# A spectral layer with two dense layers: inverse DFT constants split on chip, and a front in another order

## The chip, the cores and the metric

The kernel runs on one core of a Trainium2 chip. The metric is device time in microseconds (us). The kernel before takes 1214.83 us, the median of three runs (1214.05 to 1216.38). The engines are TensorE (PE; its weight loads are PEld), VectorE (DVE), ScalarE (ACT), GpSimd (POOL) and SyncE (SP), which here only issues transfers. DVE, ACT and POOL each take their instructions in the order in which they are written.

## The reference

The input `x` has 2 sequences of 3008 tokens with 256 features. A spectral layer comes first, then two dense layers on the 6016 tokens:

```
X  = rfft(x, axis=1)
Yr = Xr @ w_r - Xi @ w_i + b_r ;  Yi = Xr @ w_i + Xi @ w_r + b_i
Y  = soft threshold (0.01) of Yr and of Yi, each by itself
x  = irfft(Y, n=3008)
h  = x @ w_in ;   x = (h - tanh(h)) @ w_out
h  = x @ w_in2 ;  y = (h * clip(h + 3, 0, 6) / 6) @ w_out2
```

## The kernel before

A float32 operand is split into a high part `h` (rounded to the type that TensorE takes, float32r) and a low part `l`, and a product is three matmuls: h by h, h by l, l by h (`three_pass`, lines 119 to 122). The splitting is `split` (lines 115 to 117): ACT copies to the high part, DVE subtracts it from the source.

The transform of length 3008 is done in two steps, 47 by 64, and so has four matrices: `am` and `bm` forwards, `cm` and `dm` backwards. The spectral phase runs like this:

- `dft_a(i)`, i = 0 to 15 (8 for each sequence): 8 matmuls with `am` on one chunk of `x`, eviction from PSUM, and a store to DRAM (`s1`), issued by ACT. For sequence 0 the first four frequency groups are kept on the chip: they sit in partitions 96 to 127 of `xa`, and SP copies them into the ring buffer `bi_ring[0]` by 4 transfers (line 657).
- `dft_b(j)`, j = 0 to 23: two frequency groups, with the matrix `bm` (tile `bmt`, loaded in 6 groups of 256 KB), out of a ring of three buffers `bi_ring` that `load_bi` fills from `s1`. `dft_b(2)` is the first that needs `load_bi(1)` and the second group of `bm`.
- ACT and DVE split its result: `evict_b_hi` (ACT, `fh`), `evict_b_lo` (DVE, `fl`), `evict_b_neg` (ACT, a negated copy inside `fl`).
- `linear(j)`: 24 matmuls with the split weights `lwH`, `lwL`. Then `shrink` (bias and soft threshold: three operations of DVE, lines 349 to 351), `shrink_hi` (ACT, `sh`) and `shrink_lo` (DVE, `sl`).
- `dft_c(j)`: 12 matmuls with `cm` (two tiles, `cmH` and `cmL`, 6 groups of columns each), `evict_c` on ACT (`co`), and a store to `s2`. `dft_d` comes later.

The loop over t = 0 to 23 (line 679) issues `linear(t)`, `dft_c(t-2)`, `dft_b(t+2)` and, while there are chunks left, one `dft_a` for TensorE; and in this order for the other engines: `evict_c(t-2)`, `evict_b_hi(t+2)`, `shrink(t)`, `shrink_hi(t)`, `evict_b_lo(t+2)`, `evict_b_neg(t+2)`, three steps of weight decoding, `shrink_lo(t)`, the eviction and store of `dft_a`, loads, three more steps of decoding. The schedule is written by hand (`tc.manual_schedule`, line 615), so this is the order on each engine.

The weights of the dense layers come as 64-bit floats. `w_steps` (lines 164 to 210) rebuilds float32 out of the integer words and splits it, in small steps that are spread over the loop. A tile takes two operations on ACT (lines 174, 175), then on DVE lines 177, 187 and 199, for a tile of `w_in` also four small additions (lines 203 to 207), and its split one step of the next tile later (ACT line 184, DVE line 192). Tiles of `w_in` (896 columns in the split) and of `w_out` (512) alternate.

In the kernel before, `cm` comes from DRAM in both parts: line 626 loads a group's high and its low part, 256 KB each, on POOL's queue, behind a small copy (`gate`, line 624) that holds the load back until its turn.

The dense phase (`group`, lines 570 to 613) follows; the change does not touch it.

Of the kernel before, what the change touches and what calls it, by code (L numbers as in the profile page):

```python
# [20 lines left out]
K1 = 24  # L21
# [6 lines left out]
def dft_constants():  # L28
    def trig(idx, period):
        idx = np.asarray(idx, dtype=np.int64) % period  # L30
        a = 2.0 * np.pi * idx.astype(np.float64) / period
        c, s = np.cos(a), np.sin(a)
        s[(2 * idx) % period == 0] = 0.0
        c[(4 * idx) % period == 0] *= (2 * idx[(4 * idx) % period == 0]) % period == 0
        return c, s

    n1 = np.arange(N1)
    k1 = np.arange(K1)
    c, s = trig(n1[:, None] * k1[None, :], N1)
    am = np.zeros((N1, 2, K1, 2, 2))  # L40
    dm = np.zeros((K1, 2, 2, N1, 2))
    wt = np.where(k1 == 0, 1.0, 2.0) / SEQ
    for par in range(2):
        am[:, par, :, 0, par] = c
        am[:, par, 1:, 1, par] = -s[:, 1:]
        dm[:, 0, par, :, par] = (c * wt).T
        dm[1:, 1, par, :, par] = (-s * wt).T[1:]

    n2 = np.arange(N2)
    k2 = np.arange(N2)  # L50
    k = k1[:, None] + N1 * k2[None, :]
    sgn = np.where(k <= SEQ // 2, 1.0, -1.0)
    cb, sb = trig(n2[:, None, None] * k[None], SEQ)
    bm = np.zeros((2, N2, K1, 2, N2))
    bm[0, :, :, 0, :] = cb
    bm[1, :, :, 0, :] = sb
    bm[0, :, :, 1, :] = -sgn * sb
    bm[1, :, :, 1, :] = sgn * cb
    cm = np.zeros((2, N2, K1, 2, N2))
    ct = cb.transpose(2, 1, 0)  # L60
    st = sb.transpose(2, 1, 0)
    sg = sgn.T[:, :, None]
    cm[0, :, :, 0, :] = ct
    cm[1, :, :, 0, :] = -sg * st
    cm[0, :, :, 1, :] = st
    cm[1, :, :, 1, :] = sg * ct
    f = np.float32

    def round_r(v):
        u = v.astype(f).view(np.uint32)  # L70
        u = (u + np.uint32(0x7FF) + ((u >> np.uint32(12)) & np.uint32(1))) & np.uint32(0xFFFFF000)
        return u.view(f)

    am96 = np.zeros((96, 128))
    am96[0:94, 0:96] = am.reshape(94, 96)
    am96[0:94, 96:128] = am.reshape(94, K1, 4)[:, 0:8].transpose(0, 2, 1).reshape(94, 32)
    cm = cm.reshape(128, K1 * 128).astype(f)
    ch = round_r(cm)
    cl = round_r(cm - ch)
    return {  # L80
        "am": am96.astype(f),
        "bm": bm.reshape(128, K1 * 128).astype(f),
        "cm": np.stack([ch, cl], axis=1),
        "dm": dm.reshape(96, 94).astype(f),
    }

# [2 lines left out]
def spectral_moe_kernel(ctx: ExitStack, tc: tile.TileContext, x, w_r, w_i, b_r, b_i,  # L89
# [46 lines left out]
        W[nm, c] = pl.tile([128, 2, n], F32R, tag=f"w{kind}{c}", name=f"w{kind}{c}")  # L136
        return W[nm, c]

    A0 = 9
    NDEC = 13  # L140
    w_src = {"1i": w1i, "1o": w1o, "2i": w2i, "2o": w2o}
    w_order = [(nm, c) for c in range(8) for nm in ("1i", "1o")]
# [136 lines left out]
    def dft_a_out(i, banks_):  # L279
# [6 lines left out]
                act.activation(out=xt[:, 2 * g:2 * g + 2, :], in_=banks_[g], func=ACTF.Copy)  # L286
        act.dma_start(out=s1w[b][:, 4 * c:4 * c + 4, :], in_=xt[0:96])

    bi_t, xf_t, s_t = {}, {}, {}
    GB = 4  # L290

# [323 lines left out]
    with tc.manual_schedule():  # L615
# [6 lines left out]
        def load_cm(g, after):  # L622
            if g < 6:
                pool.tensor_copy(out=gate[0:1, 0:1], in_=after)
                for h, t in enumerate((cmH, cmL)):
                    pool.dma_start(out=t[:, 512 * g:512 * g + 512], in_=cm[:, h, 512 * g:512 * g + 512])

        sp.dma_start(out=amt, in_=am)
        for i in range(8):
            load_x(i)  # L630
        warm = ca.tile([128, 256], F32, name="warm")
        dve.memset(warm, 0.0)
        for _ in range(4):
            p = bank("h")
            pe.matmul(out=p[:, 0:256], lhsT=warm[:, 0:128], rhs=warm, start=True, stop=True)
        for r in range(3):
            pool.memset(x1[r][64:96], 0.0)
        dve.memset(three, 3.0)
# [3 lines left out]
            sp.dma_start(out=t, in_=w.rearrange("(h p) d -> p h d", p=128))  # L642
            lws.append(t)
        load_bm(0)
        load_x(8)
        w_load()
        for k, w in enumerate((b_r, b_i)):
            sp.dma_start(out=bias[64 * k:64 * k + 64, 0, :],
                         in_=w.rearrange("(o d) -> o d", o=1).broadcast_to([64, D]))
        for i in range(A0):  # L650
            dft_a(i)
            if i == 5:
                for k in range(2):
                    split(lwH[:, k], lwL[:, k], lws[k])
            if i == 7:
                for k in range(GB):
                    sp.dma_start(out=bi_ring[0][:, k, :], in_=xa[96 + k:128:8])
                bi_t[0] = bi_ring[0]
        load_x(9)
        load_bi(1)  # L660
        load_bm(1)
        load_x(10)
        w_load()
        sp.dma_start(out=dmt, in_=dm)
        for _ in range(5):
            w_step()
        wa_cm.__exit__(None, None, None)
        wpool["r"] = ctx.enter_context(tc.tile_pool(name="wr", bufs=1, side="right", reuse_waits="tile"))
        for j in range(2):
# [1 line left out]
            evict_b_hi(j)  # L671
            evict_b_lo(j)
            evict_b_neg(j)
            if j == 0:
                load_cm(0, xf_t[0][0].bitcast(F32)[0:1, 0, 64:65])
        load_bi(2)
        NP = K1
        a_next = A0
        for t in range(NP):
# [7 lines left out]
                evict_c(t - 2)  # L687
            if t + 2 < NP:
                evict_b_hi(t + 2)
            shrink(t)  # L690
            if t < NP - 1:
                shrink_hi(t)
# [6 lines left out]
            if t + 2 < NP:  # L699
                evict_b_neg(t + 2)  # L700
            for _ in range(3 if t < 10 else 2):
                if t > 1 and ptr["dec"] < NDEC:
                    w_step()
            shrink_lo(t)
            for nm in {20: ("b11", "b21"), 21: ("t1",), 22: ("t2", "b22")}.get(t, ()):
# [9 lines left out]
            if t % 2 == 0:  # L715
                load_bm(t // 2 + 2)
                load_cm(t // 2 + 1, s_t[t][0].bitcast(F32)[0:1, 0, 0:1])
            load_x(11 + t)
            if t == 0:
                w_load()  # L720
            if t % 2 == 1:
                load_bi((t + 1) // 2 + 2)
            for _ in range(3 if t < 10 else 1 + t % 2):
                if t > 1 and ptr["dec"] < NDEC:
                    w_step()
            if t == 14:
                load_din(0, din0)
# [122 lines left out]
```

## Time and profile before

| | |
|---|---|
| median of three runs | 1214.83 us |
| the profiled execution | 1212.14 us |
| its span (first to last instruction) | 1210.3 us |
| PE busy | 1185.4 us (98%) |
| DVE busy | 965.6 us (80%) |
| ACT busy | 875.2 us (72%) |
| POOL busy | 157.2 us (13%) |

The profile's page lists busy time over the whole span. The spectral phase is the first 170 us or so of it; the timeline lists single instructions, and a bracket at a row's end says how long the engine stood idle before it and what ended the wait. "PEclk" is the clock that TensorE was granted, as a share of its upper level of 2.4 GHz.

### The profile page before, as it was taken

To read this page: it belongs to the slowest core of one execution; us is meant where nothing else is said; L and a number is where in the kernel's file an instruction comes from. 1 tells how busy PE (TensorE), PEld (TensorE's weight loads), DVE (VectorE), ACT (ScalarE), POOL (GpSimd) and SP (SyncE) were. 2 spreads that over 40 slices of the span, in tenths; PEclk is the share of its full clock that TensorE was granted. 3 is DMA by queue.
4 is the path that set the end of the run, shared out by engine and by line. 5 is a ranking of instruction groups with operands and counts; after the bars stand their busy time and mean duration, and the time that the engine had idled before them with its cause. 6 is when DMAs were issued, how large, how long until landed. Compare 5 with 4: busy or idle time off the path is not lost.

```text
span 1210.3 us, 20904 instructions
## 1 busy us (share of the span) xinstructions
PE 1185.4 (98%) x7832; PEld 1164.5 (96%) x7832; DVE 965.6 (80%) x1820; ACT 875.2 (72%) x1827; POOL 157.2 (13%) x162
## 2 busy tenths in 40 slices
PE   7989999999999999999999999999999999999998
PEld 5888989999999999999999999999999999999998
DVE  2589988888988888888777787878787878787875
ACT  2576678777777777777777677777777777776765
POOL 0100000203020110202021402011020202020200
PEclk8899999999999999999999999999999999999999
DMA  9996621112232223120105530101010101010000
GB/s 292 284 308 187 205 87 44 41 70 74 92 105 74 75 75 100 57 82 25 51 1 196 178 111 1 52 1 52 1 52 1 53 1 52 1 29 24 14 14 26
DMA packets 47797, 96.52 MB, mean 80 GB/s; under 512 B 4352, under 2 KB 27488, under 8 KB 47696
## 3 DMA queue, kind: packets, MB, share of 16 engines
q1 hardware_dynamic: 41728, 74.09, 19.2%
q0 software_dynamic: 4032, 14.68, 3.8%
q10 hardware_dynamic: 1936, 6.42, 1.4%
q8 instruction: 61, 1.00, 0.3%
q14 instruction: 40, 0.33, 0.1%
HBM read 58.22 MB, written 36.44 MB: 78 GB/s over the span
## 4 chain that ended last, share of the span: by engine, by line
PE 73%; DVE 11%; ACT 11%; DMA 2%; issue 2%; SPq 0%; ACTq 0%; DVEq 0%
PE acc L122 13%; PE acc L120 13%; PE acc L121 13%; PE al L120 6%; PE al L121 6%; PE al L122 6%; PE be L122 3%; PE be L121 3%; PE be L120 3%; ACT gh L116 3%; DVE g L447 3%; PE ga L405 2%; DVE gl L117 2%; PE ga L121 1%; PE ga L122 1%
## 5 line engine op out<-in xcount | busy, mean ns | idle before, releaser
L117 DVE TENSOR_TENSOR gl<-g,gh 128x376 fp32r<-128x376 f32 x509 | 292.2, 574 | 149.6 <-ACT gh L116 123.2
L116 ACT ACTIVATE gh<-g 128x376 fp32r<-128x376 f32 x509 | 263.4, 517 | 176.7 <-DVE g L450 91.5
L122 PE MATMUL acc<-wo,gl 128*128 128x256 f32 (+1 forms) x768 | 215.9, 281 | 0.0
L121 PE MATMUL acc<-wo,gh 128*128 128x256 f32 (+1 forms) x768 | 215.8, 281 | 0.0
L120 PE MATMUL acc<-wo,gh 128*128 128x256 f32 (+1 forms) x768 | 215.6, 281 | 0.0
L120 PE MATMUL acc<-gh,wo 128*128 128x376 f32 x512 | 173.2, 338 | 0.0
L122 PE MATMUL acc<-gh,wo 128*128 128x376 f32 x512 | 171.0, 334 | 0.0
L121 PE MATMUL acc<-gl,wo 128*128 128x376 f32 x512 | 170.7, 333 | 0.0
L121 PEld LDWEIGHTS acc<-wo,gh 128*128 128x128 f32 (+1 forms) x768 | 143.0, 186 | 0.0
L122 PEld LDWEIGHTS acc<-wo,gl 128*128 128x128 f32 (+1 forms) x768 | 142.9, 186 | 0.0
L120 PEld LDWEIGHTS acc<-wo,gh 128*128 128x128 f32 (+1 forms) x768 | 142.8, 186 | 0.0
L414 POOL TENSOR_TENSOR bmt<-bmt 128x376 f32<-128x376 f32 x60 | 73.4, 1224 | 445.5 <-ACT bmt L407 331.2
L450 DVE SCALAR_TENSOR_TENSOR g<-e,c 128x376 f32<-128x376 f32 x192 | 118.5, 617 | 12.2 <-ACT e L449 7.5
L449 ACT ACTIVATE e<-c,three 128x376 f32<-128x376 f32 x192 | 116.7, 608 | 7.7 <-DVE c L596 7.5
L447 DVE TENSOR_TENSOR g<-c,e 128x376 f32<-128x376 f32 x189 | 114.5, 606 | 5.9 <-ACT e L446 3.4
L430 POOL TENSOR_TENSOR cmL<-bmt,cmH 128x376 fp32r<-128x376 f32 x60 | 64.9, 1082 | 324.8 <-ACT cmH L425 324.8
L446 ACT ACTIVATE e<-c 128x376 f32<-128x376 f32 x189 | 97.6, 516 | 10.0 <-DVE c L596 9.8
L120 PEld LDWEIGHTS acc<-gh,wo 128*128 128x128 f32 x512 | 96.3, 188 | 0.0
L121 PEld LDWEIGHTS acc<-gl,wo 128*128 128x128 f32 x512 | 96.2, 188 | 0.0
L122 PEld LDWEIGHTS acc<-gh,wo 128*128 128x128 f32 x512 | 96.1, 188 | 0.0
L586 ACT ACTIVATE s<-be 128x376 f32<-128x376 f32 x127 | 61.8, 487 | 40.5 <-PE be L122 39.9
L120 PE MATMUL al<-cmH,wi 128*128 128x376 f32 x256 | 87.3, 341 | 2.1 <-ACT s L582 0.3
(173 smaller groups left out, 2831.2 us busy)
## 6 DMA issues: line engine op xcount, KB each, us to landing
raw<-in_moe_w_in_dram SPq DMA_DIRECT2D x16, 512.0 KB, 3.9
raw<-in_moe_w_out_dram SPq DMA_DIRECT2D x16, 512.0 KB, 4.2
w2id<-wout SPq DMA_DIRECT2D x8, 896.0 KB, 4.7
wi<-w2id POOLq DMA_DIRECT2D x8, 896.0 KB, 4.9
y1d<-y SPq DMA_DIRECT2D x32, 188.0 KB, 2.0
bmt<-y1d SPq DMA_DIRECT2D x8, 752.0 KB, 4.5
s<-co SPq DMA_DIRECT2D x23, 256.0 KB, 4.6
bi_all<-s SPq DMA_DIRECT2D x11, 512.0 KB, 5.1
```

Source lines behind the costliest of these rows:

```text
L116: act.activation(out=hi, in_=src, func=ACTF.Copy)
L117: (lo_eng or dve).tensor_tensor(out=lo, in0=src, in1=hi.bitcast(F32), op=ALU.subtract)
L120: pe.matmul(out=out_ap, lhsT=lh, rhs=rh, start=start, stop=False, **kw)
L121: pe.matmul(out=out_ap, lhsT=lh, rhs=rl, start=False, stop=False, **kw)
L122: pe.matmul(out=out_ap, lhsT=ll, rhs=rh, start=False, stop=stop, **kw)
L414: eng.tensor_tensor(out=out, in0=a, in1=b, op=ALU.subtract)
L430: (eng or dve).tensor_tensor(out=l, in0=OPS[nm][0], in1=h.bitcast(F32), op=ALU.subtract)
L446: act.activation(out=e, in_=src, func=ACTF.Tanh)
L447: dve.tensor_tensor(out=g, in0=src, in1=e, op=ALU.subtract)
L449: act.activation(out=e, in_=src, func=ACTF.Relu, bias=three)
L450: dve.scalar_tensor_tensor(out=g, in0=e, scalar=6.0, in1=src, op0=ALU.min, op1=ALU.mult)
L586: act.activation(out=s5, in_=be, func=ACTF.Copy)
```

## The change

Three things change together.

1. `cm` is one float32 array in DRAM. `load_cm` loads a group of 256 KB into one of two buffers `cmf`, and a new function `split_cm(g)` splits it on ACT and DVE into `cmH` and `cmL`. It is called at t = 1, 3, 5, 7, 9 and 11, ahead of `shrink(t)`. The gate of the first group is now the first of the four copies into `bi_ring[0]`.
2. The front is in another order. `A0` is 8 instead of 9, so `dft_a(8)` moves into the loop, and the loop does one more `dft_a` (t = 0 to 7). The split of `lwH`, `lwL` moves from between the evictions of `dft_a` to behind them. On SP the four copies into `bi_ring[0]` come ahead of the two bias loads, `load_x(8)`, `load_bi(1)` and the first `w_load`. Eleven matmuls on a tile of zeros (`warm`) stand between `dft_a(7)` and `dft_b(0)`. `warm` has 240 columns instead of 256.
3. The five decoding steps ahead of the loop are gone; decoding starts at t = 1 instead of t = 2.

```diff
@@ -66,21 +66,13 @@
     cm[1, :, :, 1, :] = sg * ct
     f = np.float32
 
-    def round_r(v):
-        u = v.astype(f).view(np.uint32)
-        u = (u + np.uint32(0x7FF) + ((u >> np.uint32(12)) & np.uint32(1))) & np.uint32(0xFFFFF000)
-        return u.view(f)
-
     am96 = np.zeros((96, 128))
     am96[0:94, 0:96] = am.reshape(94, 96)
     am96[0:94, 96:128] = am.reshape(94, K1, 4)[:, 0:8].transpose(0, 2, 1).reshape(94, 32)
-    cm = cm.reshape(128, K1 * 128).astype(f)
-    ch = round_r(cm)
-    cl = round_r(cm - ch)
     return {
         "am": am96.astype(f),
         "bm": bm.reshape(128, K1 * 128).astype(f),
-        "cm": np.stack([ch, cl], axis=1),
+        "cm": cm.reshape(128, K1 * 128).astype(f),
         "dm": dm.reshape(96, 94).astype(f),
     }
 
@@ -136,7 +128,7 @@
         W[nm, c] = pl.tile([128, 2, n], F32R, tag=f"w{kind}{c}", name=f"w{kind}{c}")
         return W[nm, c]
 
-    A0 = 9
+    A0 = 8
     NDEC = 13
     w_src = {"1i": w1i, "1o": w1o, "2i": w2i, "2o": w2o}
     w_order = [(nm, c) for c in range(8) for nm in ("1i", "1o")]
@@ -286,6 +278,7 @@
                 act.activation(out=xt[:, 2 * g:2 * g + 2, :], in_=banks_[g], func=ACTF.Copy)
         act.dma_start(out=s1w[b][:, 4 * c:4 * c + 4, :], in_=xt[0:96])
 
+    cmf = {}
     bi_t, xf_t, s_t = {}, {}, {}
     GB = 4
 
@@ -622,17 +615,22 @@
         def load_cm(g, after):
             if g < 6:
                 pool.tensor_copy(out=gate[0:1, 0:1], in_=after)
-                for h, t in enumerate((cmH, cmL)):
-                    pool.dma_start(out=t[:, 512 * g:512 * g + 512], in_=cm[:, h, 512 * g:512 * g + 512])
+                cmf[g] = ca.tile([128, 512], F32, tag="cmf", bufs=2, name="cmf")
+                pool.dma_start(out=cmf[g], in_=cm[:, 512 * g:512 * g + 512])
+
+        def split_cm(g):
+            if g < 6:
+                sl = slice(512 * g, 512 * g + 512)
+                split(cmH[:, sl], cmL[:, sl], cmf[g])
 
         sp.dma_start(out=amt, in_=am)
         for i in range(8):
             load_x(i)
-        warm = ca.tile([128, 256], F32, name="warm")
+        warm = ca.tile([128, 240], F32, name="warm")
         dve.memset(warm, 0.0)
         for _ in range(4):
             p = bank("h")
-            pe.matmul(out=p[:, 0:256], lhsT=warm[:, 0:128], rhs=warm, start=True, stop=True)
+            pe.matmul(out=p[:, 0:240], lhsT=warm[:, 0:128], rhs=warm, start=True, stop=True)
         for r in range(3):
             pool.memset(x1[r][64:96], 0.0)
         dve.memset(three, 3.0)
@@ -642,28 +640,28 @@
             sp.dma_start(out=t, in_=w.rearrange("(h p) d -> p h d", p=128))
             lws.append(t)
         load_bm(0)
-        load_x(8)
-        w_load()
+        for i in range(A0):
+            dft_a(i)
+        for k in range(GB):
+            sp.dma_start(out=bi_ring[0][:, k, :], in_=xa[96 + k:128:8])
+        bi_t[0] = bi_ring[0]
         for k, w in enumerate((b_r, b_i)):
             sp.dma_start(out=bias[64 * k:64 * k + 64, 0, :],
                          in_=w.rearrange("(o d) -> o d", o=1).broadcast_to([64, D]))
-        for i in range(A0):
-            dft_a(i)
-            if i == 5:
-                for k in range(2):
-                    split(lwH[:, k], lwL[:, k], lws[k])
-            if i == 7:
-                for k in range(GB):
-                    sp.dma_start(out=bi_ring[0][:, k, :], in_=xa[96 + k:128:8])
-                bi_t[0] = bi_ring[0]
+        load_x(8)
+        load_bi(1)
+        w_load()
         load_x(9)
-        load_bi(1)
         load_bm(1)
+        sp.dma_start(out=dmt, in_=dm)
         load_x(10)
         w_load()
-        sp.dma_start(out=dmt, in_=dm)
-        for _ in range(5):
-            w_step()
+        load_cm(0, bi_ring[0][0:1, 0, 0:1])
+        for k in range(2):
+            split(lwH[:, k], lwL[:, k], lws[k])
+        for _ in range(11):
+            p = bank("h")
+            pe.matmul(out=p[:, 0:240], lhsT=warm[:, 0:128], rhs=warm, start=True, stop=True)
         wa_cm.__exit__(None, None, None)
         wpool["r"] = ctx.enter_context(tc.tile_pool(name="wr", bufs=1, side="right", reuse_waits="tile"))
         for j in range(2):
@@ -671,8 +669,6 @@
             evict_b_hi(j)
             evict_b_lo(j)
             evict_b_neg(j)
-            if j == 0:
-                load_cm(0, xf_t[0][0].bitcast(F32)[0:1, 0, 64:65])
         load_bi(2)
         NP = K1
         a_next = A0
@@ -687,6 +683,8 @@
                 evict_c(t - 2)
             if t + 2 < NP:
                 evict_b_hi(t + 2)
+            if t % 2 and t < 12:
+                split_cm(t // 2)
             shrink(t)
             if t < NP - 1:
                 shrink_hi(t)
@@ -699,7 +697,7 @@
             if t + 2 < NP:
                 evict_b_neg(t + 2)
             for _ in range(3 if t < 10 else 2):
-                if t > 1 and ptr["dec"] < NDEC:
+                if t > 0 and ptr["dec"] < NDEC:
                     w_step()
             shrink_lo(t)
             for nm in {20: ("b11", "b21"), 21: ("t1",), 22: ("t2", "b22")}.get(t, ()):
@@ -715,13 +713,14 @@
             if t % 2 == 0:
                 load_bm(t // 2 + 2)
                 load_cm(t // 2 + 1, s_t[t][0].bitcast(F32)[0:1, 0, 0:1])
-            load_x(11 + t)
+            if t > 0:
+                load_x(10 + t)
             if t == 0:
                 w_load()
             if t % 2 == 1:
                 load_bi((t + 1) // 2 + 2)
             for _ in range(3 if t < 10 else 1 + t % 2):
-                if t > 1 and ptr["dec"] < NDEC:
+                if t > 0 and ptr["dec"] < NDEC:
                     w_step()
             if t == 14:
                 load_din(0, din0)
```

Line numbers of the changed file are lower by 8 in what follows (line 349 before is line 342 or so after). The first place is DVE, at the end of iteration t = 2 and the start of t = 3. `raw` and `ws` belong to the decoding, `ly` and `lc` to `shrink`. Before:

```order
L177 TENSOR_SCALAR raw<-raw 128x512
L187 SCALAR_TENSOR_TENSOR ws<-ws,raw 128x512
L361 TENSOR_TENSOR sl<-ly,sh 128x512
L192 TENSOR_TENSOR wi_464<-ws,wi_464 128x896
L199 ISA ws<-ws 128x1024
L349 TENSOR_TENSOR ly<-acc,bias 128x512
L350 TENSOR_SCALAR lc<-ly 128x512
L351 TENSOR_TENSOR ly<-ly,lc 128x512
L322 TENSOR_TENSOR fl<-be,fh 128x4x128
```

After:

```order
L169 TENSOR_SCALAR raw<-raw 128x512
L179 SCALAR_TENSOR_TENSOR ws<-ws,raw 128x512
L184 TENSOR_TENSOR wi_477<-ws,wi_477 128x896
L354 TENSOR_TENSOR sl<-ly,sh 128x512
L191 ISA ws<-ws 128x1024
L169 TENSOR_SCALAR raw<-raw 128x512
L109 TENSOR_TENSOR cmL<-cmf,cmH 128x512
L342 TENSOR_TENSOR ly<-acc,bias 128x512
L343 TENSOR_SCALAR lc<-ly 128x512
L344 TENSOR_TENSOR ly<-ly,lc 128x512
L315 TENSOR_TENSOR fl<-al,fh 128x4x128
```

The subtraction for `cmL` stands at the head of the odd iteration, ahead of `shrink`; and the decoding is one step further along, so that a `raw` operation ends the even iteration instead of opening the next batch.

The second place is ACT in the same stretch, from the negated copy (`fl<-fl`) of the even iteration to `sh` of the odd one. Before:

```order
L327 ACTIVATE fl<-fl 128x4x64
L174 ACTIVATE ws<-raw 128x512
L175 ACTIVATE ws<-raw 128x512
L184 ACTIVATE wi_464<-ws 128x896
L286 ACTIVATE xb_98<-ga 96x512
L286 ACTIVATE xb_98<-al 96x512
L287 DMA s_1_61<-xb_98 96x1024
L174 ACTIVATE ws<-raw 128x512
L175 ACTIVATE ws<-raw 128x512
L379 ACTIVATE co<-acc 128x512
L315 ACTIVATE fh<-be 128x4x128
L316 ACTIVATE fh<-be 128x4x64
```

After:

```order
L176 ACTIVATE wi_477<-ws 128x896
L278 ACTIVATE xb_100<-al 96x512
L278 ACTIVATE xb_100<-be 96x512
L279 DMA s_1_61<-xb_100 96x1024
L166 ACTIVATE ws<-raw 128x512
L167 ACTIVATE ws<-raw 128x512
L176 ACTIVATE wo_499<-ws 128x512
L372 ACTIVATE co<-acc 128x512
L308 ACTIVATE fh<-al 128x4x128
L309 ACTIVATE fh<-al 128x4x64
L108 ACTIVATE cmH<-cmf 128x512
L350 ACTIVATE sh<-ly 128x512
```

The new copy `cmH<-cmf` comes behind `co` and the two `fh` of the odd iteration; one pair of decoding copies (lines 174, 175 before) has gone from ahead of `wi`, and the split of the next tile (`wo_499`) has moved in behind the other pair.

The third place is SP's queue behind the first group of `bm`. Before:

```order
L620 DMA bmt<-in_bm_dram 128x512
L257 DMA xb_98<-in_x_dram 80x1024
L257 DMA xb_98<-in_x_dram 14x1024
L158 DMA raw<-in_moe_w_in_dram 128x2x256
L648 DMA bias<-in_b_r_dram 64x256
L648 DMA bias<-in_b_i_dram 64x256
L657 DMA bi_all<-xa 128x1x256 x4
L257 DMA xb_99<-in_x_dram 80x1024
L257 DMA xb_99<-in_x_dram 14x1024
L297 DMA bi_all<-s_0_60 128x4x256
L620 DMA bmt<-in_bm_dram 128x512
```

After:

```order
L646 DMA bi_all<-xa 128x1x256 x4
L649 DMA bias<-in_b_r_dram 64x256
L649 DMA bias<-in_b_i_dram 64x256
L249 DMA xb_98<-in_x_dram 80x1024
L249 DMA xb_98<-in_x_dram 14x1024
L290 DMA bi_all<-s_0_60 128x4x256
L150 DMA raw<-in_moe_w_in_dram 128x2x256
L249 DMA xb_99<-in_x_dram 80x1024
L249 DMA xb_99<-in_x_dram 14x1024
L613 DMA bmt<-in_bm_dram 128x512
```

The four copies have moved up past a chunk of `x`, a weight tile and the bias; the second group of `bm` now has all of these between the copies and itself.

## Rows read from the trace of the kernel before

**Rows 1.** Busy time of each engine, granted clock and DMA in the loop's middle.

```profile
core 0: us, PE busy (x) PEld busy (x) DVE busy (x) ACT busy (x) POOL busy (x), PEclk, DMA share, GB/s
...
53.30:132.40 79.10, 72.84 (x570) 69.28 (x568) 71.55 (x130) 55.65 (x109) 5.15 (x12) 1.00 0.80 246
```

**Rows 2.** TensorE's waits from 53.3 to 132.4 us: total, times, longest.

```profile
PE acc L122 <- DVE fl L322: 2.0, 3, 1.5
```

**Rows 3.** Timeline of VectorE and ScalarE, iterations t=6, 7: start, length, line, operation.

```profile
78.42 0.68 DVE L349 TENSOR_TENSOR ly<-acc,bias 128x512 f32<-128x512 f32 x1
...
80.31 0.69 DVE L322 TENSOR_TENSOR fl<-al,fh 128x512 fp32r<-128x512 f32 x1
...
81.03 0.42 ACT L327 ACTIVATE fl<-fl 128x256 fp32r<-128x256 f32 x1
...
82.04 0.43 DVE L177 TENSOR_SCALAR raw<-raw 128x512 uint32<-128x512 uint32 x1 [1.04 <-ACT ws L174]
82.49 0.94 ACT L184 ACTIVATE wi<-ws 128x896 fp32r<-128x896 f32 x1
...
83.34 0.58 ACT L286 ACTIVATE xb<-ga 96x512 f32<-96x512 f32 x1
...
84.43 0.31 ACTq L287 DMA_DIRECT2D s<-xb  x1
...
84.84 0.69 ACT L174 ACTIVATE ws<-raw 128x512 f32<-128x512 f32 x1 [0.44 <-DVE wi L192]
...
85.33 0.68 DVE L349 TENSOR_TENSOR ly<-acc,bias 128x512 f32<-128x512 f32 x1
...
86.01 0.58 ACT L379 ACTIVATE co<-acc 128x512 f32<-128x512 f32 x1
...
86.49 0.59 ACT L315 ACTIVATE fh<-be 128x512 fp32r<-128x512 f32 x1
...
87.23 0.64 ACT L357 ACTIVATE sh<-ly 128x512 fp32r<-128x512 f32 x1
87.38 0.69 DVE L322 TENSOR_TENSOR fl<-be,fh 128x512 fp32r<-128x512 f32 x1 [0.18 <-ACT fh L316]
...
88.43 0.62 ACT L184 ACTIVATE wo<-ws 128x512 fp32r<-128x512 f32 x1
...
91.95 0.68 DVE L349 TENSOR_TENSOR ly<-acc,bias 128x512 f32<-128x512 f32 x1
```

**Rows 4.** Timeline: the first operation of shrink at t=1, 2 and 15.

```profile
45.27 0.69 DVE L349 TENSOR_TENSOR ly<-acc,bias 128x512 f32<-128x512 f32 x1 [2.21 <-PE acc L122]
...
50.75 0.69 DVE L349 TENSOR_TENSOR ly<-acc,bias 128x512 f32<-128x512 f32 x1 [2.22 <-PE acc L122]
...
129.91 0.68 DVE L349 TENSOR_TENSOR ly<-acc,bias 128x512 f32<-128x512 f32 x1
```

**Rows 5.** Timeline of the front: TensorE, ScalarE and SyncE's transfer issues.

```profile
17.51 1.89 PE L273 MATMUL acc<-xa,amt 96*128 96x256 f32 x8
...
21.87 0.60 ACT L286 ACTIVATE xa<-acc 128x512 f32<-128x512 f32 x1 [1.36 <-DVE xa L284]
...
23.43 4.15 SPq L657 DMA_DIRECT2D bi_all<-xa  x4
...
31.79 0.50 SPq L620 DMA_DIRECT2D bmt<-in_bm_dram  x1
...
34.29 1.22 PE L308 MATMUL ga<-bmt,bi_all 128*128 128x128 f32 x4 [1.40 <-DMA bi_all<-xa]
...
39.58 0.61 PE L308 MATMUL al<-bmt,bi_all 128*128 128x128 f32 x4
```

**Rows 6.** SyncE's waits from 36 to 42 us: total, times, longest.

```profile
SPq L620 <- DMA bmt<-in_bm_dram: 2.2, 1, 2.2
```

**Rows 7.** Timeline: the price of one split on ScalarE and VectorE, two each.

```profile
18.88 1.15 ACT L116 ACTIVATE lwH<-lwf 128x512 fp32r<-128x512 f32 x2 [0.39 <-ACT xa L286]
19.54 1.29 DVE L117 TENSOR_TENSOR lwL<-lwf,lwH 128x512 fp32r<-128x512 f32 x2 [2.86 <-ACT lwH L116]
```

## The prediction, made before the changed kernel ran

> **What bounds the kernel now.** I read the busy time by stretches first, then the waits, then the timeline of the stretch that the change touches, the spectral phase. Behind it the dense phase is TensorE's own work, which the change leaves alone, so that a shift at the end of the spectral phase is a shift of the kernel. In the loop's middle VectorE works 71.55 of 79.10 us, ScalarE 55.65 [rows 1]. VectorE's rows stand back to back there: from shrink at t=6 to shrink at t=8 it takes 13.53 us, and of these it idles only 1.04 us before its `raw` operation, for ScalarE's decoding copy, and 0.18 us before `fl`, for ScalarE's `fh` [rows 3]. TensorE needs less: where its waits are for results, the named one is VectorE's `fl`, and it is short, 2.0 us in all [rows 2], because TensorE runs ahead and is held back once an iteration. So from t=2 to t=15 the clock of this phase is VectorE's queue, and where VectorE stands at t=15 (129.91 us, [rows 4]) says when TensorE can go on alone. I follow two numbers: when `dft_b(2)` starts (39.58 us now, [rows 5]), and how long VectorE needs from there to shrink at t=15, now 129.91 - 39.58 = 90.3 us.
>
> **The front.** Before the loop, the last link is the second group of `bm`: SyncE issued it at 31.79 us [rows 5], and a later issue that reuses its completion slot waited 2.2 us until it had landed, at 39.3 [rows 6]; `dft_b(2)` started at 39.58. What the new order does to that:
> - The last eviction of `dft_a(7)` starts at 21.87 us behind a wait of 1.36 us that comes from the split of `lwL` (1.29 us for both halves, ahead of VectorE's copy) [rows 5, 7]. With the split behind the evictions it ends 1.3 us earlier, at 21.2 instead of 22.5 (bounds 20.5 and 22.5: the store of a chunk may still hold ScalarE). The four copies then start at 21.2 instead of 23.43.
> - In the kernel before the last copy was awaited until 34.29, 10.9 us after the first was issued [rows 5], behind a chunk of `x`, a weight tile and the bias, 0.38 + 0.52 + 0.13 = 1.03 MB by the tile shapes. From 34.29 to 39.3 the transfers behind it were `x(9)`, `load_bi(1)`, the `bm` group, `cm` in two parts and one store, 0.38 + 0.52 + 0.26 + 0.52 + 0.39 = 2.07 MB in 5.0 us, 0.41 MB per us. At that rate 1.03 MB are 2.5 us, so the copies end 8.4 us after their start, at 29.6 (bounds: 4.15 us of issue plus little, 26; and the 10.9 as now, 32).
> - Now more stands between them and the `bm` group: the bias, `x(8)`, `load_bi(1)`, a weight tile, `x(9)`, the group itself and half of the old `cm`: 0.13 + 0.38 + 0.52 + 0.52 + 0.38 + 0.26 + 0.26 = 2.45 MB, 5.9 us. That gives 35.5 us for `dft_b(2)`; I take 35.3 (range 33 to 38.5), 4.3 us earlier than now.
>
> The Trainium skill, page "DMA: Bandwidth & Descriptors", section "Why a DMA increments its semaphore by 16 and not by 1", says that a transfer runs on as many of the 16 DMA engines as divide its slowest dimension; a copy out of 4 partitions would run on 4. With that page's figure of about 27 GiB/s for one engine, an estimate for one copy of 128 KB is 1.1 us, 4.5 for four; the sum would then be about 2 us smaller. The rows of this case show the four landing only over 10.9 us, with others in the queue, so the trace neither bears it out nor excludes it.
>
> The eleven warm matmuls lie in TensorE's wait: `dft_a` runs 8 passes of 256 columns in 1.89 us [rows 5], so 22 passes of 240 columns take 4.5 us from 19.4, to 23.9; the copies land later (at half that rate they would end at 28.4, still before the last copy). Price nothing; with copies at 26 and the slow rate, 2 us. The first `warm` matmuls, shorter by a sixteenth, I price at nothing (bounds 0 and 2 us, if TensorE's clock came up later; the copies' wait would hide part). `dft_a(8)` in the loop costs nothing where VectorE sets the pace.
>
> **The loop.** One split costs VectorE 1.29 / 2 = 0.65 us and ScalarE 1.15 / 2 = 0.58 us [rows 7]; six are 3.9 us of VectorE. What matters more is where they stand. The subtraction is at the head of an odd iteration, ahead of `shrink`; it needs ScalarE's `cmH`, which stands behind `co` and the two `fh` of the same iteration. VectorE takes nothing out of turn, so `shrink`, `fl`, the decoding and `sl` all queue behind it, and TensorE waits for these.
>
> At t=1 VectorE is not yet late. Now `shrink(1)` starts when `linear(1)` ends, 45.27 - 39.58 = 5.7 us after `dft_b(2)` [rows 4, 5]. After, it must wait for `dft_b(3)` (0.9 us, as 8 passes of 0.11), the two `fh` (0.74, from 86.49 to 87.23), `cmH` 0.58 and `cmL` 0.65 [rows 3, 7]: 2.9 us, say 3.0. Then shrink(1) to shrink(2) is 5.48 us now [rows 4]; after, decoding starts here: shrink 1.87 (85.33 to 87.38, less 0.18), then from `fl` to the next shrink 4.57 as at t=7 (87.38 to 91.95), less 0.6 for a subtraction that has no tile yet, plus the 1.04 wait [rows 3]: 6.9, so +1.4. Together +4.4 at shrink(2).
>
> From t=2 on, a pair of iterations. In the even one, from the start of `fl`: VectorE has `fl` 0.69, then what now runs from 82.04 to 85.33 (3.29) and one more `raw` operation 0.45, so it reaches `cmL` after 4.4 us. ScalarE has, behind `fl`, the negated copy 0.42 (starting 0.72 after `fl`), `wi` 0.85 (82.49 to 83.34), the evictions and store of `dft_a` 1.50 (83.34 to 84.84), the decoding copies 1.17 (84.84 to 86.01), `wo` 0.52 (0.62 by its row, which overlaps the next by 0.1), `co` 0.48 (86.01 to 86.49), `fh` 0.74, `cmH` 0.58 [rows 3, 7]: 0.72 + 6.26 = 7.0 us. VectorE waits 2.6 us. Against that the 1.04 us for the `raw` operation goes, since its copies now run half an iteration earlier, and the 0.18 us too. A pair changes by 0.65 + 2.6 - 1.04 - 0.18 = +2.0 us. There are three (t=2 to 7): +6.0; the first also loses a 0.6 us wait for `fh` that the kernel before had there: +5.4. At t=8 `dft_a` is over and ScalarE is 1.50 us shorter, the wait 1.1: +0.5. At t=10 to 14, one more split with a wait of some 0.5 us against a 1.04 wait less: about +0.1. So +6.0 from shrink(2) to shrink(15), bounds -3.4 (no wait at any split: 7.8 + 1.1 + 0.5 = 9.4 us of waits less) and +8.
>
> Sum: -4.3 + 4.4 + 6.0 = +6.1 us at t=15; TensorE goes on alone from there. In the profiled execution 1212.14 becomes 1218.2; the median of the runs shown lies 2.7 us higher, so 1220.9. Halving the bytes of `cm` is already in the 2.45 MB; in the loop it earns nothing, as VectorE and ScalarE set the pace there.
>
> **Rivals.**
> - The other side: ScalarE stays ahead, so that `cmH` is always there. It would need to reach `cmH` 2.6 us earlier in each odd iteration. Against it: `fl` already waits 0.18 us for `fh` in the kernel before, 1.87 us further down VectorE's queue than the split stands [rows 3]. For it: the phase of the decoding moves, and ScalarE has some 25 us free in 79 [rows 1]. Then the loop gives -3.4 instead of +6.0, and the kernel -3.3: 1211.5. It turns where the wait is 1.0 us instead of 2.6.
> - Half of it: waits of some 1.3 us; about +1.4, 1216.2, no difference.
> - VectorE's lateness doesn't reach TensorE: the waits named for it are only 2.0 us [rows 2]. Then only the front counts, with the 3.0 of the first split against 4.3: about -1.3, or up to -4: no difference or faster, 1211 to 1214.
> - The front is not earlier at all (the copies' wait stays 10.9 us and the larger queue takes its 5.9): `dft_b(2)` at 38 to 39.5, +9 to +10, 1224.
>
> **How the numbers follow.** The forecast 0.48, the late front 0.15, half the wait 0.15, ScalarE ahead 0.14, no reach 0.08. About 0.2% of the time, 2.4 us, is what a measurement tells from no change. Faster: ScalarE ahead and most of no reach, 0.20. Same: half the wait and a little from each side, 0.18. Slower 0.62. For 8 in 10 I leave out the fastest tenth, below 1212.5, and the slowest, above 1225.5 (the late front with full waits).
>
> **What would show it.** Right: VectorE idle about 2 to 3 us before `cmL` at t=3, 5 and 7, named for ScalarE's `cmH`, about 1 at t=9, and a pair of iterations of 15.5 us; `raw` without its 1.04 wait; `dft_b(2)` at 33 to 38. Wrong: `cmL` rows without a wait, shrink at t=15 before 129.9 us, or TensorE's waits unchanged though VectorE is late. A granted clock at half in the loop would be something I have not priced.

## The result and the profile after

The changed kernel takes 1226.89 us, the median of four runs (1223.72 to 1228.09), against 1214.78 for the kernel before; the ratio is 1.0093 (95% interval 1.008 to 1.0107). The direction and the loop's mechanism were forecast, the front's was not: the prediction was 1220.9, with a range that ended at 1225.5. The line numbers of the changed kernel are 7 or 8 lower than in the kernel before (shrink's first operation is L342, `dft_b` L301, the split's two operations L108 and L109).

The profiled execution's span grew from 1210.3 to 1221.9 us, by 11.6. Both profiled executions (1212.14 us before, 1223.72 after) lie some 3 us below their medians. From the page of the changed kernel:

```profile
span 1221.9 us, 20946 instructions
...
PE 1193.0 (98%) x7854; PEld 1172.3 (96%) x7854; DVE 967.2 (79%) x1825; ACT 879.2 (72%) x1834; POOL 154.7 (13%) x156
```

The two times to follow are again the start of `dft_b(2)` and the first operation of shrink at t=15. First the front, in the timeline (start, length, engine, line, operation, idle time before it):

```profile
20.40 4.40 SPq L646 DMA_DIRECT2D bi_all<-xa  x4
...
25.76 0.68 PE L301 MATMUL ga<-bmt,bi_all 128*128 128x128 f32 x4 [1.71 <-issue]
...
30.44 1.23 PE L301 MATMUL al<-bmt,bi_all 128*128 128x128 f32 x4 [0.81 <-DMA bi_all<-xa]
...
30.80 0.74 SPq L613 DMA_DIRECT2D bmt<-in_bm_dram  x1
...
39.59 0.37 SPq L150 DMA_DIRECT2D raw<-in_moe_w_in_dram  x1
39.66 2.05 PE L301 MATMUL be<-bmt,bi_all 128*128 128x128 f32 x8 [3.15 <-issue]
```

The four copies start 3 us earlier than in [rows 5] and the last one is awaited until 30.44 instead of 34.29, yet `dft_b(2)` starts at 39.66, where it started before (39.58). TensorE had finished `linear(0)` at 36.5 and now waits 3.15 us, while the second group of `bm`, issued at 30.80, lands. The row's bracket names no transfer. SyncE's waits do: its issue at 39.59 had waited for this group and comes free at the same moment (total, times, longest), and in e9_bm_mid below the bracket names it too.

```profile
SPq L150 <- DMA bmt<-in_bm_dram: 1.1, 1, 1.1
```

From issue to landing the `bm` load takes 8.8 us. The same front in stretches (length, busy times, granted clock, mean DMA share, GB/s), copies first, then what is behind them:

```profile
20.40:30.44 10.04, 5.86 (x31) 4.66 (x30) 1.98 (x3) 2.44 (x5) 0.80 (x2) 0.94 0.73 255
30.44:39.60 9.16, 6.08 (x28) 5.87 (x28) 2.50 (x4) 1.29 (x3) 0.00 (x0) 0.69 1.03 269
```

Then shrink, in VectorE's timeline at t=1 (with the first split ahead of it), t=2 and t=15:

```profile
49.25 0.69 DVE L109 TENSOR_TENSOR cmL<-cmf,cmH 128x512 fp32r<-128x512 f32 x1 [5.25 <-ACT cmH L108]
49.86 0.68 DVE L342 TENSOR_TENSOR ly<-acc,bias 128x512 f32<-128x512 f32 x1
...
56.82 0.68 DVE L342 TENSOR_TENSOR ly<-acc,bias 128x512 f32<-128x512 f32 x1
...
141.49 0.68 DVE L342 TENSOR_TENSOR ly<-acc,bias 128x512 f32<-128x512 f32 x1
```

Against [rows 4] shrink is 4.6 us later at t=1, 6.1 at t=2 and 11.6 at t=15 (141.49 - 129.91), the whole of the span's difference. A pair of iterations in the middle, VectorE and ScalarE in one timeline, t=6 to the start of t=8:

```profile
86.92 0.68 DVE L342 TENSOR_TENSOR ly<-acc,bias 128x512 f32<-128x512 f32 x1
...
88.71 0.68 DVE L315 TENSOR_TENSOR fl<-ga,fh 128x512 fp32r<-128x512 f32 x1
...
89.43 0.42 ACT L320 ACTIVATE fl<-fl 128x256 fp32r<-128x256 f32 x1
89.75 0.94 ACT L176 ACTIVATE wi<-ws 128x896 fp32r<-128x896 f32 x1
...
92.93 0.42 DVE L169 TENSOR_SCALAR raw<-raw 128x512 uint32<-128x512 uint32 x1
...
94.25 0.59 ACT L308 ACTIVATE fh<-al 128x512 fp32r<-128x512 f32 x1
...
94.99 0.64 ACT L108 ACTIVATE cmH<-cmf 128x512 fp32r<-128x512 f32 x1
95.66 0.69 DVE L109 TENSOR_TENSOR cmL<-cmf,cmH 128x512 fp32r<-128x512 f32 x1 [2.30 <-ACT cmH L108]
96.26 0.68 DVE L342 TENSOR_TENSOR ly<-acc,bias 128x512 f32<-128x512 f32 x1
...
101.98 0.68 DVE L342 TENSOR_TENSOR ly<-acc,bias 128x512 f32<-128x512 f32 x1
```

ScalarE's queue from `fl` to `cmH` (88.71 to 95.6, 6.9 us) is what the prediction added up as 7.0. VectorE is at `cmL` after 4.65 us and stands for 2.30. The `raw` operation at 92.93 has lost its wait of [rows 3]. The pair takes 15.06 us; it took 13.53. VectorE's waits from 40 to 140 us (total, times, longest), where the one of 4.3 us is that for `dft_b(2)`, and the others, six at `cmL` above all, are the loop's:

```profile
DVE cmL L109 <- ACT cmH L108: 14.7, 6, 5.3
DVE fl L315 <- ACT fh L309: 4.3, 1, 4.3
DVE raw L169 <- ACT ws L166: 1.0, 1, 1.0
DVE wi L184 <- ACT wi L176: 1.0, 4, 0.3
```

From t=2 to 15 VectorE is busy 72.91 us of 84.67, ScalarE 58.07: neither is at its limit, and the two wait for each other in turn.

```profile
56.82:141.49 84.67, 74.83 (x543) 70.40 (x542) 72.91 (x136) 58.07 (x115) 2.89 (x8) 0.94 0.76 238
```

The granted clock of this stretch is 0.94, where it was 1.00 in [rows 1]. It was 0.66 from 80 to 85 us, for example, after TensorE had waited 2.65 us for a chunk of `x`. The pairs don't show it: the one with these 5 us took 15.05 us, the next, at 1.00, 15.06.

### The profile page after: what moved, and what is told of

Its sections match the earlier page's. It is cut to its first block, busy times and chain, and to the rows that moved or that the text cites. A ratio compares the mean times of both kernels' runs of the same rounds, so it can differ in the third digit from the quotient of the medians.

```text
span 1221.9 us, 20946 instructions
## 1 busy us (share of the span) xinstructions
PE 1193.0 (98%) x7854; PEld 1172.3 (96%) x7854; DVE 967.2 (79%) x1825; ACT 879.2 (72%) x1834; POOL 154.7 (13%) x156
## 4 chain that ended last, share of the span: by engine, by line
PE 71%; DVE 12%; ACT 12%; DMA 2%; issue 2%; SPq 0%; ACTq 0%; DVEq 0%
PE acc L112 12%; PE acc L114 12%; PE acc L113 12%; PE al L112 6%; PE al L113 6%; PE al L114 6%; PE be L114 3%; PE be L113 3%; PE be L112 3%; ACT gh L108 3%; DVE g L440 2%; PE ga L398 2%; DVE gl L109 2%; PE ga L113 1%; PE ga L114 1%
## 5 line engine op out<-in xcount | busy, mean ns | idle before, releaser
L109 DVE TENSOR_TENSOR gl<-g,gh 128x376 fp32r<-128x376 f32 x509 | 291.4, 573 | 149.4 <-ACT gh L108 123.1
L108 ACT ACTIVATE gh<-g 128x376 fp32r<-128x376 f32 x509 | 263.4, 518 | 176.6 <-DVE g L443 91.6
L579 ACT ACTIVATE s<-be 128x376 f32<-128x376 f32 x127 | 61.8, 487 | 39.6 <-PE be L114 39.2
```

The source lines that it names most:

```text
L108: act.activation(out=hi, in_=src, func=ACTF.Copy)
L109: (lo_eng or dve).tensor_tensor(out=lo, in0=src, in1=hi.bitcast(F32), op=ALU.subtract)
L579: act.activation(out=s5, in_=be, func=ACTF.Copy)
```

## The experiments

The first of the four copies is issued at 20.4 to 23.0 us in the eight profiled kernels with the new front, earliest in the changed kernel itself. So the traces are compared by distances: from the matmul that awaits the last copy to `dft_b(2)`, from there to shrink at t=1, and from there to shrink at t=15. All in us from one profiled execution; "clock" is the granted clock in the 5 us from `dft_b(2)` on. Each ratio is to executions of the kernel before that were taken beside that kernel.

| kernel | median | ratio to before (95%) | last copy to `dft_b(2)` | its wait | clock | to shrink, t=1 | to shrink, t=15 |
|---|---|---|---|---|---|---|---|
| before | 1214.41 to 1215.37 | 1 | 5.3 | none | 1.00 | 5.7 | 90.3 |
| after | 1226.89 | 1.0093 (1.008, 1.0107) | 9.2 | 3.15 | 0.68 | 10.2 | 101.8 |
| e1_split_late | 1219.15 | 1.003 (1.0017, 1.0042) | 9.8 | 5.33 | 0.50 | 8.5 | 94.5 |
| e2_bm_early | 1219.54 | 1.0041 (1.0026, 1.0056) | 5.9 | 0.21 | 1.00 | 8.6 | 100.3 |
| e3_split_only | 1227.28 | 1.0105 (1.009, 1.012) | 5.4 | none | 1.00 | 8.6 | 104.2 |
| e4_front_only | 1214.77 | 1.0005 (0.9995, 1.0015) | 10.2 | 4.34 | 0.50 | 8.1 | 89.5 |
| e5_front_bm | 1208.13 | 0.9946 (0.9934, 0.9958) | 6.1 | none | 0.99 | 5.6 | 88.0 |
| e6_late_bm | 1212.31 | 0.998 (0.9971, 0.9988) | 6.4 | 1.92 | 1.00 | 5.6 | 91.0 |
| e7_no_warm | 1226.08 | 1.0092 (1.0079, 1.0105) | 9.1 | 3.47 | 0.50 | 11.4 | 103.1 |
| e8_before_bm | 1214.35 | 1.0005 (0.9991, 1.0019) | 6.0 | none | 1.00 | 5.7 | 89.9 |
| e9_bm_mid | 1221.42 | 1.0048 (1.0027, 1.0069) | 5.5 | 0.90 | 1.00 | 8.6 | 100.3 |

**The split in another place.** The same work, called later in the iteration:

```
-            if t % 2 and t < 12:
-                split_cm(t // 2)
             shrink(t)
...
+            if t % 2 and t < 12:
+                split_cm(t // 2)
             shrink_lo(t)
```

> The changed kernel with the call of split_cm moved, in the same odd iterations, from ahead of shrink(t) to just ahead of shrink_lo(t). The work is the same, only its place in VectorE's and ScalarE's queues differs. Theory 1 (place): VectorE's waits before cmL (5.25 us at t=0/1, then 2.29, 2.28, 2.30, 2.12 and 0.41) go, and with them most of the loss of the loop: 8 to 12 us faster than the changed kernel, within 4 us of the kernel before. Theory 2 (amount): the six splits and the five decoding steps are simply too much work for VectorE and ScalarE in the loop; then moving the call only shifts the waits to other rows and gains less than 3 us.

The median fell by 7.7 us against the changed kernel, a little less than expected, though in the profiled execution the front came late (`dft_b(2)` at 42.35). From there to t=15 the loop got 7.3 us shorter: the waits at `cmL` are gone at t=1 to 9, and one of 1.51 us stays at t=11. Against e4_front_only below, which has no split, the split costs 12.1 us in the changed kernel, so most of its price was its place and not its work.

**The `bm` group first.** One line moved in the changed kernel:

```
         load_bm(0)
+        load_bm(1)
...
         load_x(9)
-        load_bm(1)
```

> The changed kernel with the second group of bm loaded right behind the first (SyncE stands idle there from 13.5 to 20.4 us), instead of behind load_x(9). Theory 1 (the queue order sets the end of the front): dft_b(2), now at 39.66 us, is then released by load_bi(1), issued at 28.74, and starts at 34 to 37; 2.5 to 5 us faster than the changed kernel, since everything behind it in the loop keeps its length. Theory 2 (all of the front's transfers share one rate, so that load_bi(1) or x(8) comes as late as the bm group does): dft_b(2) stays at 38 to 40 and the time within 1.5 us.

7.35 us faster than the changed kernel, more than the 2.5 to 5 expected. `dft_b(2)` starts at 36.69, 5.9 us behind the last copy, and the granted clock is full from there on. The two stretches of 5 us from `dft_b(2)`, first in the changed kernel:

```profile
39.66:44.66 5.00, 5.00 (x23) 4.33 (x24) 1.29 (x2) 2.61 (x6) 1.19 (x2) 0.68 0.97 319
```

and in this one:

```profile
36.69 1.13 PE L301 MATMUL be<-bmt,bi_all 128*128 128x128 f32 x8 [0.21 <-DMA bi_all<-s]
...
36.69:41.69 5.00, 5.00 (x36) 4.60 (x37) 2.93 (x5) 2.77 (x6) 1.19 (x2) 1.00 1.02 269
```

Both are fully busy, but 23 matmuls fit in the first and 36 in the second. In the rest of the loop nothing changed: the pair takes 15.05 us, with waits of 2.27 to 2.30 us. So what the distances show of the gain is 3.3 us up to `dft_b(2)` and 1.6 behind it, where the clock was low. The other 2.4 us of the 7.35 they don't show. The changed kernel's profiled execution is 3.2 us below its median, and e7_no_warm, with the same queue, shows a clock of 0.50 where it shows 0.68; whether its other executions look like that one is not shown.

**One half alone.** The kernel before with nothing but the new `cm` and its split ahead of shrink (and the `warm` tile of 240 columns):

```
-                for h, t in enumerate((cmH, cmL)):
-                    pool.dma_start(out=t[:, 512 * g:512 * g + 512], in_=cm[:, h, 512 * g:512 * g + 512])
+                cmf[g] = ca.tile([128, 512], F32, tag="cmf", bufs=2, name="cmf")
+                pool.dma_start(out=cmf[g], in_=cm[:, 512 * g:512 * g + 512])
...
+            if t % 2 and t < 12:
+                split_cm(t // 2)
             shrink(t)
```

> The kernel before with the new cm alone: one float32 load per group, split_cm at t=1,3,..,11 ahead of shrink(t), 240 columns in warm; front and decoding as before. Theory 1 (place): cmL waits for cmH behind the two fh here too. In the kernel before fh ended 2.05 us after the start of shrink in odd iterations, so waits of 2.6 us or more at t=3,5,7,9 and about 3 at t=1: 8 to 13 us slower than the kernel before. Theory 2 (front and decoding made the loss): 1 to 4 us slower (six subtractions of 0.65 us).

And the other half: the new front and the earlier decoding, with `cm` from DRAM in both parts as before (the reverse of that diff, in the changed kernel).

> The changed kernel with cm loaded from DRAM in both parts as before (two loads of 256 KB for each group, no split on chip); front and decoding as changed. Theory 1 (place): without the splits the loop is paced by VectorE's other work, 12.3 to 12.9 us for a pair of iterations instead of 15.05; dft_b(2) stays near 39.7 us or comes up to 1 us later (0.26 MB more in the queues): 0 to 4 us faster than the kernel before. Theory 2 (front and decoding made the loss): 6 to 11 us slower than the kernel before.

The split alone costs 12.9 us against the kernel before, as much as the whole change. Its waits from 43 to 146 us:

```profile
DVE cmL L109 <- ACT cmH L108: 15.8, 6, 4.5
DVE raw L169 <- ACT ws L166: 5.2, 5, 1.0
```

Here both waits stand, the new one at `cmL` and the old one at `raw`: the pair takes 16.3 us (70.31 to 86.60). The prediction's credit of 1.04 us for `raw` is thus the earlier decoding's, as it said. The front and the decoding alone made no difference: a loop 0.8 us shorter, behind a `dft_b(2)` at 41.78 that waited 4.34 us.

**Both repairs, and a version without the split.** First e4_front_only with the `bm` line of e2_bm_early:

> The front and the earlier decoding with cm still loaded in both parts (as in e4_front_only), and the second group of bm moved up to stand right behind the first in SyncE's queue. Theory (what ended the front was this group's place in the queue, and the half clock followed from the wait): dft_b(2) at 36 to 38 us without a wait of more than 0.3 us, granted clock full again from about 36 us, 88 to 90 us from there to shrink at t=15, so 126 instead of 131.3; about 1209 to 1211 us, faster than the kernel before by 0.3% or more. Rival (the transfers share one rate, so an early group only delays the four copies by its own 0.6 us and the loads behind it): dft_b(2) at 40 or later and 1214 us, no change from e4_front_only. Rival (VectorE's lateness does not reach TensorE once the front is short): the shrink at t=15 is early but the time stays at 1214.

Then the changed kernel with the late split and the early `bm` group:

> The changed kernel with both repairs: the split of cm just ahead of shrink_lo(t) (as in e1_split_late) and the second group of bm right behind the first (as in e2_bm_early). If the two losses are independent, the gains add: e1 gained about 7.5 us and e2 about 7 against the changed kernel, so 1212 to 1213 us, about the kernel before or 0.2% faster; dft_b(2) near 37 us, some 93 to 94 us from there to shrink at t=15, cmL without a wait of over 0.5 us in t=1 to 9. If both were one loss seen twice (the half clock after a late start, say), the sum is less: 1217 or more. Against e5_front_bm it should be 3 to 4 us slower, the six subtractions on VectorE (0.65 us each), if the split costs its own work and no more.

e5_front_bm is the fastest kernel of the study, just below the time expected, 6.6 us below e4_front_only and 0.54% below the kernel before. From its timeline:

```profile
37.99 1.09 PE L308 MATMUL be<-bmt,bi_all 128*128 128x128 f32 x8
...
125.95 0.69 DVE L349 TENSOR_TENSOR ly<-acc,bias 128x512 f32<-128x512 f32 x1
```

`dft_b(2)` waits for nothing, 1.6 us earlier than before, and shrink at t=15 is 4.0 us earlier; the span fell by 3.8 us (1206.5). e6_late_bm shows that the two losses add: 14.6 us below the changed kernel, 7.7 and 7.35 alone. A pair of it, t=7 to the start of t=8, in VectorE's timeline:

```profile
82.07 0.68 DVE L342 TENSOR_TENSOR ly<-acc,bias 128x512 f32<-128x512 f32 x1
...
85.74 0.69 DVE L191 CUSTOM_DVE_ANT_0 ws<-ws 128x1024 uint16<-128x1024 uint16 x1
86.34 0.69 DVE L109 TENSOR_TENSOR cmL<-cmf,cmH 128x512 fp32r<-128x512 f32 x1
86.94 0.68 DVE L354 TENSOR_TENSOR sl<-ly,sh 128x512 fp32r<-128x512 f32 x1
...
88.48 0.68 DVE L342 TENSOR_TENSOR ly<-acc,bias 128x512 f32<-128x512 f32 x1
```

`cmL` runs without a wait, since `cmH` is long done by then. Its distance to t=15 is 91.0 us, less than the 93 to 94 expected, and 3.0 us longer than that of e5_front_bm. Six subtractions of 0.6 us and the 1.51 us at t=11 make 5.1; against them stand 2.0 us of waits that are shorter here (those for `fh` and for `acc` behind t=1 are 2.8 us in all in e5_front_bm, and 0.8 in this kernel). By the medians the split costs 4.2 us even here, and nothing in these runs pays for it.

**The eleven warm matmuls.** The changed kernel without them; they compute nothing that is used:

```
-        for _ in range(11):
-            p = bank("h")
-            pe.matmul(out=p[:, 0:240], lhsT=warm[:, 0:128], rhs=warm, start=True, stop=True)
```

> The changed kernel without the eleven warm matmuls behind dft_a; they compute nothing that is used. Theory (they lie inside TensorE's wait for the four copies, price nothing): time within 1.5 us of the changed kernel's, dft_b(2) within 1 us of its 39.7 once the start of the copies is compared. Rival (they hold the clock at its upper level until 28.5 us): without them the granted clock falls ahead of the first dft_b, and shrink at t=1 is 1 us or more later, 1228 to 1229 us. Rival (TensorE's extra work costs something itself): 1 to 2 us faster.

No difference (1226.08; ratio 1.0092 against 1.0093). In the stretch from 19.4 to 28.5 us the granted clock was 1.00 in the changed kernel, with TensorE busy 6.04 us. Without them:

```profile
19.40:28.50 9.10, 3.21 (x15) 2.61 (x14) 2.68 (x4) 2.94 (x5) 0.80 (x2) 0.72 0.77 301
```

So they do hold the clock up there, but it had fallen by `dft_b(2)` in both. The profiled execution is 1.2 us slower from `dft_b(2)` to shrink at t=1, which the medians don't show; whether that is the execution or the edit stays open.

**Was it the `bm` group in the kernel before?** The same line moved in the kernel before:

> The kernel before with one line moved: the second group of bm right behind the first. Reading A (the prediction's: in the kernel before dft_b(2) started when this group had landed, at 39.3 us): dft_b(2) comes earlier by up to 3 us. Reading B (there dft_b(2) stands right behind the 24 matmuls of linear(0), with no wait in its row, and those behind the last copy at 34.29 us): dft_b(2) still 5.2 to 5.4 us behind the matmul that awaits the last copy, the time within 1 us of the kernel before, 1213.5 to 1215.5 us.

No difference: 1214.35, ratio 1.0005 (0.9991 to 1.0019). From its timeline:

```profile
35.23 1.01 PE L308 MATMUL ga<-bmt,bi_all 128*128 128x128 f32 x3 [0.72 <-DMA bi_all<-xa]
...
41.13 0.27 PE L122 MATMUL acc<-lwH,fl 128*128 128x256 f32 x1
41.24 0.94 PE L308 MATMUL al<-bmt,bi_all 128*128 128x128 f32 x7
```

`dft_b(2)` follows the last matmul of `linear(0)` at once. The distance to the last copy, 6.0 us, is a little over the 5.2 to 5.4 expected and over the 5.3 of [rows 5]; no part of it is a wait for `bm`: TensorE is busy throughout, at a granted clock of 0.51 in these 6.0 us, and of 0.60 in the 5.3 us of the kernel before. Reading B holds.

**How much stands ahead of it.** In the changed kernel the `bm` group moved by two places, ahead of one weight tile and `x(9)`:

```
         load_bi(1)
+        load_bm(1)
         w_load()
         load_x(9)
-        load_bm(1)
```

> The changed kernel with the second group of bm moved by two places only, ahead of one weight tile (0.52 MB) and x(9) (0.38 MB). In the changed kernel dft_b(2) began 9.2 us behind the matmul that awaited the last copy (30.44 to 39.66), and the transfers ran at 269 GB/s in between. Theory (the group lands when the bytes ahead of it are through, at the rate of that stretch): 0.90 MB less are 3.3 us, so dft_b(2) 5.8 to 6.5 us behind that matmul, where linear(0) and load_bi(1) also end, granted clock full again by 41 us, and the time 4 to 7 us below the changed kernel's: 1220 to 1222.5. At the prediction's rate of 410 GB/s it would be 2.2 us less: 7.0 us behind. Rival (all transfers in flight share the rate and land together, so a place in the queue matters little): 8.5 us or more behind, 1225 to 1227.

1221.42 us, 5.5 less than the changed kernel. The group was issued at 31.60 and the matmul started at 37.77, 5.5 us behind that of the last copy (32.28):

```profile
37.77 1.13 PE L301 MATMUL be<-bmt,bi_all 128*128 128x128 f32 x8 [0.90 <-DMA bmt<-in_bm_dram]
```

3.7 us less than in the changed kernel, nearer to the 3.3 of 269 GB/s than to the 2.2 of the prediction's rate. It doesn't tell the two rates apart, though: with the changed kernel's queue the distance was 9.1 to 9.8 us in three executions (after, e1, e7), and from issue to landing the group took 2.6 us less (6.2 against 8.8). What it does show is that the place in the queue sets when the group lands.

## Why the prediction was right and where it failed

Profile against profile the forecast at shrink t=15 was +6.1 us; it became +11.6. The difference of 5.5 is the front's 4.4, the clock's 1.6, and -0.5 in the loop. The term that failed is the front: -4.3 us forecast, +0.1 measured.

- **The copies' start: in this execution better than forecast.** 20.40 instead of 21.2. In four other kernels with the same queue up to there (e1, e4, e7, e9) it was 22.3 to 23.0, so this one execution doesn't settle the term.
- **The copies' end: too early by 1.6 us in length.** 10.04 us from first issue to last arrival, 8.4 forecast (9.3 to 9.9 in those four kernels). Taking 1.03 MB from ahead of the copies was to save 2.5 us and saved 0.8. They landed 5.4 us after the first issue and then 1.3 to 1.7 us apart. The prediction's estimate of 1.1 us a copy, 4.5 for four, worked out from the Trainium skill, page "DMA: Bandwidth & Descriptors" (4 of the 16 engines by the section "Why a DMA increments its semaphore by 16 and not by 1", 27 GiB/s for one by the section "Specifications"), would have made it still shorter. The trace's 10.04 us do not bear it out; against 8.4 it would have been 3.9 us less, and not the 2 that the prediction gives. That the mean DMA share was only 0.73 in this stretch would go with copies on fewer engines, but no run here isolated it.
- **The bytes behind them: the step that failed.** The count fits what the stretch moved (269 GB/s for 9.16 us are 2.46 MB), the rate does not. 2.45 MB at 269 GB/s are 9.1 us, and 9.2 were measured; the prediction took 0.41 MB per us and got 5.9. That rate came from adding up the shapes of everything that was awaited between 34.29 and 39.3 us, 2.07 MB, while the view gives 1.46 MB for it (291 GB/s for 5.01 us): part had moved outside it. The same view of the kernel before has the rate, in its last column; copies first, then that stretch:

```profile
23.43:34.29 10.86, 7.20 (x20) 4.74 (x21) 4.18 (x9) 3.11 (x6) 1.36 (x3) 0.50 0.77 264
34.29:39.30 5.01, 5.01 (x26) 5.01 (x27) 0.69 (x1) 1.29 (x3) 0.00 (x0) 0.58 1.27 291
```

  With 264 to 291 GB/s the same sum gives 8.4 to 9.3 us, and `dft_b(2)` at 38.0 to 38.9: the rival "the front is not earlier at all", which was given 0.15 and 1224 us. It came there by another sum, 10.9 us for the copies and 5.9 for the queue, where 10.0 and 9.2 were measured. Put together, -0.8 at the start, +1.6 for the copies and +3.3 for the bytes move the forecast of 35.5 to 39.6, where it was found.
- **What ended the front before: misread.** The prediction took the landing of the `bm` group (39.3) for the last link ahead of `dft_b(2)` (39.58). The row in [rows 5] has no bracket: TensorE came from `linear(0)` without a pause, and e8_before_bm shows that an earlier group changes nothing. The group was merely ready in time. The change made it the last link, by taking 3.9 us from the copies and putting more bytes ahead of it. The prediction also left out TensorE's own work there: `linear(0)` ended at 36.5, 6.1 us behind the last copy, so that even with the group in place `dft_b(2)` would have come 3.1 us earlier and not 4.3 (36.69 in e2_bm_early).
- **The clock: named, and not priced.** Behind the wait of 3.15 us the clock was at half its level for part of the stretch (0.68), and shrink at t=1 came 10.2 us after `dft_b(2)`, against 8.6 in the kernels with the same split and a full clock (e2, e9). That is 1.6 us. At 0.50 it is 2.8 (11.4, e7). Without a split ahead of shrink it is 2.5 and 2.9: 8.1 (e4) against 5.6 (e5), 8.5 (e1) against 5.6 (e6).
- **The split at t=1: right.** +3.0 forecast; 8.6 against 5.6 to 5.7 us in the kernels with a full clock is 3.0. From shrink(1) to shrink(2) 6.96 us, 6.9 forecast.
- **The pairs: right, a little too long.** 15.06 us against 15.5 forecast, the wait 2.3 us against 2.6, since VectorE arrives 4.65 us after `fl`, not 4.4 (0.26 us of a wait before `wi` is in that). At t=9 the wait was 2.12 us and not 1.1, so this pair gave +1.5 and not +0.5. ScalarE had no evictions of `dft_a` left there, as forecast, but it stood 1.16 us for VectorE's `wi` instead, 0.44 in the pair before:

```profile
106.91 0.67 ACT L166 ACTIVATE ws<-raw 128x512 f32<-128x512 f32 x1 [1.16 <-DVE wi L184]
```

  From t=10 on +0.07, 0.1 forecast. From shrink(2) to shrink(15) +5.5 us, +6.0 forecast, and that is closer than its terms, by luck: the first three pairs gave 4.0 us and not 5.4, the fourth 1.0 more than forecast.
- **The warm matmuls: price nothing, right.** e7_no_warm shows no difference in the medians. Their 22 passes took 4.6 us; the prediction's own figures give 4.9 and not its 4.5, which changes nothing.
- **The rivals on the other side fell.** ScalarE was not ahead at any of the six splits; VectorE's lateness did reach TensorE, as the span moved by what shrink at t=15 moved. Halving the bytes of `cm` earned nothing that these runs show.

## What to carry to other kernels

When a sum needs the rate of a queue, read it from the bytes per second of that very stretch, since shapes of what lands in it count bytes that moved earlier; and before moving a link earlier, see whether the row behind it waited for it at all. An operation that two in-order engines share belongs where its input is already there: the same six splits cost 9.3 us more ahead of shrink than just before `shrink_lo` (100.3 against 91.0 us from `dft_b(2)` to t=15 in e2 and e6; their medians are 7.2 us apart). What a loop's first iterations need goes to the front of the queue, ahead of what is only needed later; here one moved line was worth about 7 us in three kernels (1226.89 to 1219.54, 1219.15 to 1212.31, 1214.77 to 1208.13), and nothing in a fourth where it was not the last link.

## What was not expected of the hardware

The DMA engines' mean busy share (which can exceed 1) was 1.03 while they moved 269 GB/s, from 30.44 to 39.60 us, and 1.05 with 405 GB/s in the same kernel, from 16.0 to 20.4 us:

```profile
16.00:20.40 4.40, 4.40 (x22) 3.93 (x21) 2.08 (x3) 2.39 (x4) 0.00 (x0) 1.00 1.05 405
```

Which transfers are the slow ones was not tried. And a wait ahead of `dft_b(2)` was paid twice: in the four kernels where it was 3.15 us or more, the granted clock in the next 5 us was 0.50 to 0.68, although TensorE was busy in all of them; in the seven where it was 1.92 us or less, 0.99 or 1.00. So an early group of `bm` brought 7 us where the wait for it was 3 to 5.
